# The gated stage's a and b products by one level of Strassen's algorithm on quarter blocks, with partial sums read from one pair of PSUM banks

## The chip, the cores and the metric

The kernel runs on one core of one Trainium2 chip. The metric is the device time of one execution in microseconds (us); three runs were timed and the median is taken. The engines are PE (TensorE, matmuls), ACT (ScalarE), DVE (VectorE), POOL (GpSimd) and SP, which here only issues transfers. Each engine has one queue and works through it in the order written down by the program.

## What is computed

The reference is attention with a bias, then a mixture of four experts, then a gated stage. The change touches the gated stage alone:

```python
# x: 1152 tokens x 512, the experts' output; w_a, w_b: 512 x 1536; w_out: 1536 x 512
a = x @ w_a
b = x @ w_b
return a * b @ w_out
```

## The kernel before

A matrix product keeps a high and a low part of each operand (hi, lo) and adds three PE products, hi*hi + hi*lo + lo*hi; every count of matmuls below has this factor three in it. A matmul holds 128x128 weights (stationary) and streams up to 512 columns (moving).

**Gated stage.** The 1152 tokens are cut into three chunks of 384 and the 1536 inner features into six groups of 256, taken as 2 x 3 (g, q). `ab_item` (line 745) makes one item: for each of two feature halves of 128 it computes a and b, each by `up` (line 677) as 12 matmuls of 384 columns (four blocks of the 512 inputs, times three) into one PSUM bank. ACT copies a out of its bank (line 754), DVE multiplies b with it (756), ACT and DVE split the result into hi and lo (757, 758). `out_item` (line 771) follows one item later: for each of three token tiles `down` (line 689) issues six matmuls of 512 columns; the sum over three groups q stays in the bank `z`, then ACT or DVE moves it to `acc` (782, 784), and the last ones are stored.

**Ahead of it.** `x2_item` (line 732) transposes the experts' output `acc` (36 transposes of 128x128 on PE in all) and ACT and DVE write its hi and lo into `x_hi` and `x_lo`. The weights of the gated stage arrive as 64-bit words; `convert` (line 625) turns them into hi and lo on DVE during the experts' stage and stores them to DRAM (`wz_d`), `unit64` (655) loads them into one of 11 weight buffers `w`.

**What sets the order.** The program lists operations with their dependences; `Plan.run` then makes the queue of every engine from estimated durations and priorities (`RANK`; a lower number goes first), and hands out buffers (`Room`) as earlier users finish. The queues are fixed when the kernel is built; at run time semaphores only hold an instruction back, and all that stands behind it in its queue waits too.

Of the kernel before, what the change touches and what calls it, by code (L numbers as in the profile page):

```python
# [45 lines left out]
SPLIT = True  # L46

# [178 lines left out]
def tile_kernel(ctx, tc, qd, kd, vd, cst, probs, w1r, w2r, war, wbr, wor, out):  # L226
# [43 lines left out]
    solo, attn, hp_stack = ExitStack(), ExitStack(), ExitStack()  # L270
# [3 lines left out]
    R = {z: Room() for z in "w wst h1 h2 u z q2 q k2 k v bt ptb pr rb xf sums rx hh bst asb s64 t64 hl64".split()}  # L274
# [348 lines left out]
    wz_d = dram.tile([2 * NG * NQ + NG * NQ, 2, P, 1024], F32, name="wz_d")  # L623

    def convert(src):
# [3 lines left out]
        for h in range(2):  # L629
# [59 lines left out]
    def down(w, z, h, tt, first, final, prio=RANK["fill"]):  # L689
# [5 lines left out]
        op({"PE": 6 * 226}, mm, r=[w, h], w=[z], prio=prio)  # L695
# [34 lines left out]
    X2 = [Buf(t=x_hi) for _ in range(TOK)]  # L730

    def x2_item(t):
        u = new("u", "px")
        ts = slice(t * P, (t + 1) * P)
        p4 = lambda: u.t.rearrange("p (a b) -> p a b", a=KD)

        def tr(e):
            for d in range(KD):
                nc.tensor.transpose(p4()[:, d, :], acc(t)[:, d * P:(d + 1) * P], ident)  # L739

        op({"PE": 440}, tr, r=[ACC[t]], w=[u], after=ups[t], prio=1)
# [3 lines left out]
    def ab_item(g, c, q):
        h = new("h2", "h")
        if (g, q, "a") not in WU:
            for z in "ab":
                WU[g, q, z] = unit64(UI[g, q, z])
        xs = X2[3 * c:3 * c + 3]  # L750
        for ft in range(2):
            asb = new("asb")
            pa, _ = up(WU[g, q, "a"], ft, c * CH, CH, xs, [h, asb])
            op({"ACT": 490}, lambda e, pa=pa, asb=asb: nc.scalar.copy(asb.t, pa.t[:, :CH]), r=[pa], w=[asb])
            pb, _ = up(WU[g, q, "b"], ft, c * CH, CH, xs, [h, asb])
            op({"DVE": 560}, lambda e, pb=pb, asb=asb: nc.vector.tensor_tensor(out=asb.t, in0=pb.t[:, :CH], in1=asb.t, op=ALU.mult), r=[pb], rw=[asb])  # L756
            hi = op({"ACT": 490}, lambda e, ft=ft, asb=asb: nc.scalar.copy(h.t[0][:, ft, :CH], asb.t), r=[asb], w=[h])  # L757
            op({"DVE": 560}, lambda e, ft=ft, asb=asb: nc.vector.tensor_tensor(out=h.t[1][:, ft, :CH], in0=asb.t, in1=f(h.t[0][:, ft, :CH]), op=ALU.subtract), r=[asb], w=[h], after=[hi], lock=True)  # L758
        return h
# [11 lines left out]
    def out_item(g, c, q, h):  # L771
        if (g, q, "d") not in WU:
            WU[g, q, "d"] = unit64(UI[g, q, "d"])
        for tt in range(3):
            t = 3 * c + tt
            if q == 0:
                ZB[g, c, tt] = new("z", "pz")
            z = ZB[g, c, tt]
            down(WU[g, q, "d"], z, h, tt, q == 0, q == NQ - 1)
            if q == NQ - 1:  # L780
                if g == 0:
                    op({"ACT": 600}, lambda e, z=z, t=t: nc.scalar.copy(acc(t), z.t), r=[z], rw=[ACC[t]])
                else:
                    op({"DVE": 745}, lambda e, z=z, t=t: nc.vector.tensor_tensor(out=acc(t), in0=z.t, in1=acc(t), op=ALU.add), r=[z], rw=[ACC[t]])
                    if g == NG - 1:
                        def put(e, t=t):
                            for r, o, n in rows_of(t):
                                nc.sync.dma_start(out=out[o:o + n, :], in_=acc(t)[r:r + n])
                        op({"SP": 440 * len(rows_of(t))}, put, r=[ACC[t]], size=262144)
# [12 lines left out]
    def chain(items, fu, fd, at=()):  # L802
        prev = None
        for n, key in enumerate(items):
            for t in dict(at).get(n, ()):
                x2_item(t)
            h = fu(*key)
            if prev is not None:
                fd(*prev)
            prev = (*key, h)  # L810
        fd(*prev)

    for p, its in enumerate(PASSES):
        chain([(p, e, c, q) for e in range(E) for c in its for q in range(4)], w1_item, w2_item)
    UI = {}
    for g in range(NG):
        for q in range(NQ):
            for z, src in ("a", war), ("b", wbr), ("d", wor):
                UI[g, q, z] = convert(src[NQ * g + q])
    for t in range(TOK):  # L820
        x2_item(t)
    chain([(g, c, q) for g in range(NG) for c in range(NCH) for q in range(NQ)], ab_item, out_item)


# [25 lines left out]

    ended = lambda o: o.done
# [3 lines left out]
        (lambda: R["bst"].left == 0 and R["hh"].left == 0, bias_end),  # L855
        (lambda: all(o.done for o in fins) and not R["s"].left and not R["tv"].left, attn_end),
# [7 lines left out]
def _layout(q, k, v, w1, b1, w2, moe_domain_probs, moe_w1, moe_w2, moe2_w_a, moe2_w_b, moe2_w_out):  # L864
# [24 lines left out]

    def down(w, n):  # L890
# [36 lines left out]
```

## Time and profile before

| | |
|---|---|
| median of three runs (lowest, highest) | 845.51 us (843.58, 845.67) |
| the profiled execution: its time, its span | 845.99 us, 844.2 us |
| busy in the span: PE, DVE, ACT, POOL | 818.1, 540.2, 327.2, 46.4 us |
| PE busy, 626.33 to 831.60 us (gated stage) | 205.27 of 205.27 us |
| DVE and ACT busy in that stretch | 39.87 and 36.38 us |

The span runs from the first to the last instruction. Matmuls overlap in PE's pipeline, so PE's busy time says that it was never idle, not how fast it went; how fast is read from the distance between the starts of matmuls.

### The profile page before, as it was taken

What the parts mean: (1) busy time and instruction counts of PE and PEld (TensorE: products, weight loads), DVE (VectorE), ACT (ScalarE), POOL (GpSimd) and SP (SyncE); (2) the same over time, 40 slices, a digit from 0 to 9 for tenths busy, and PEclk for the clock granted to TensorE, in tenths of its full rate; (3) what the DMA queues carried; (4) which work ended last, traced back from release to release, by engine and by line L of the source; (5) the groups of instructions that cost most, each with busy time, mean ns of one, the idle gap of its engine ahead of it and who ended that gap; (6) DMA issues with size and microseconds to landing.
All of it is one profiled execution on the core that took longest, in us unless ns stands there. A gap on an engine that the chain in (4) does not pass through costs nothing.

```text
span 844.2 us, 12285 instructions
## 1 busy us (share of the span) xinstructions
PE 818.1 (97%) x4712; PEld 686.2 (81%) x4712; DVE 540.2 (64%) x1052; ACT 327.2 (39%) x640; POOL 46.4 (5%) x53
## 2 busy tenths in 40 slices
PE   6788999999999999999999999999999999999997
PEld 2446776898898788889888888888899999999996
DVE  7998999788888777787978787782421211212222
ACT  6676877577676622332232222121211221211111
POOL 1001100000110000001001000110000000000000
PEclk9999999999999999999999999999999999999999
DMA  6889877576656364566466656746510006201001
GB/s 222 308 272 335 279 253 242 196 237 189 222 174 211 119 228 167 175 207 203 139 228 195 185 160 198 265 140 209 189 51 0 1 1 249 100 1 38 1 38 38
DMA packets 53243, 140.69 MB, mean 167 GB/s; under 512 B 5312, under 2 KB 9408, under 8 KB 53184
## 3 DMA queue, kind: packets, MB, share of 16 engines
q1 hardware_dynamic: 53184, 139.90, 50.7%
q8 instruction: 37, 0.61, 0.3%
q14 instruction: 22, 0.18, 0.1%
HBM read 107.75 MB, written 32.13 MB: 166 GB/s over the span
## 4 chain that ended last, share of the span: by engine, by line
PE 91%; DVE 5%; DMA 3%; issue 1%; ACT 1%; POOL 0%; SPq 0%; DVEq 0%; POOLq 0%
PE up L685 42%; PE pz L694 33%; PE ps L489 5%; PE pv L580 4%; PE pt L515 4%; PE pb L369 2%; DVE hh L355 1%; DMA k<-in_kd 1%; DMA bt<-bias_d 1%; DVE pr L492 1%; DVE ptb L233 1%; PE rp L560 0%; PE px L739 0%; PE pt L532 0%; DMA cs<-in_cst 0%
## 5 line engine op out<-in xcount | busy, mean ns | idle before, releaser
L685 PE MATMUL up<-x_hi,wh 128*128 128x384 f32 (+2 forms) x672 | 230.0, 342 | 0.4 <-DVE hl L711 0.4
L685 PE MATMUL up<-x_hi,wl 128*128 128x384 f32 (+2 forms) x672 | 226.6, 337 | 0.0
L685 PE MATMUL up<-x_lo,wh 128*128 128x384 f32 (+2 forms) x672 | 226.4, 337 | 0.0
L694 PE MATMUL pz<-wh,hh 128*128 128x512 f32 x396 | 157.6, 398 | 0.6 <-ACT hh L757 0.6
L694 PE MATMUL pz<-wl,hh 128*128 128x512 f32 x396 | 156.1, 394 | 0.0
L694 PE MATMUL pz<-wh,hl 128*128 128x512 f32 x396 | 155.8, 393 | 0.1
L685 PEld LDWEIGHTS up<-x_hi,wh 128*128 128x128 f32 x672 | 126.4, 188 | 10.1 <-issue 1.6
L685 PEld LDWEIGHTS up<-x_lo,wh 128*128 128x128 f32 x672 | 126.5, 188 | 6.9
L685 PEld LDWEIGHTS up<-x_hi,wl 128*128 128x128 f32 x672 | 126.4, 188 | 5.7
L756 DVE TENSOR_TENSOR asb<-up,asb 128x384 f32<-128x384 f32 x36 | 20.1, 558 | 144.7 <-PE up L685 144.7
L710 ACT ACTIVATE hh<-up 128x256 fp32r<-128x256 f32 (+2 forms) x96 | 47.1, 491 | 139.5 <-PE up L685 132.2
L694 PEld LDWEIGHTS pz<-wl,hh 128*128 128x128 f32 x396 | 74.3, 188 | 17.2
L694 PEld LDWEIGHTS pz<-wh,hh 128*128 128x128 f32 x396 | 74.5, 188 | 16.2 <-ACT hh L757 1.0
L618 DVE TENSOR_TENSOR wl<-wst,wh 128x1024 fp32r<-128x1024 f32 x64 | 77.8, 1220 | 15.2 <-ACT wh L233 14.9
L694 PEld LDWEIGHTS pz<-wh,hl 128*128 128x128 f32 x396 | 74.4, 188 | 15.1 <-DVE hl L758 0.4
L711 DVE SCALAR_TENSOR_TENSOR hl<-up,hh 128x256 fp32r<-128x256 f32 (+2 forms) x96 | 52.9, 553 | 41.5 <-ACT hh L710 41.0
L233 ACT CAST wh<-wst 128x1024 fp32r<-128x1024 f32 x55 | 57.3, 1045 | 45.8 <-PE pz L694 38.0
L492 DVE CUSTOM_DVE_ANT_0 pr<-ps,bt 128x576 f32<-128x576 f32 (+1 forms) x80 | 59.7, 753 | 12.1 <-PE ps L489 8.5
L502 ACT ACTIVATE pr<-pr,sums 128x576 f32<-128x576 f32 x72 | 55.9, 776 | 12.2 <-DVE sums L492 11.5
L757 ACT CAST hh<-asb 128x384 fp32r<-128x384 f32 x36 | 18.5, 513 | 100.8 <-DVE asb L756 100.8
L369 PE MATMUL pb<-hh,cs 128*32 128x288 f32 (+17 forms) x352 | 47.0, 499 | 6.8 <-DVE hh L355 4.5
L355 DVE TENSOR_SCALAR hh<-cs,negb 128x576 f32<-128x576 f32 (+17 forms) x108 | 49.0, 503 | 0.2
(89 smaller groups left out, 873.3 us busy)
## 6 DMA issues: line engine op xcount, KB each, us to landing
wz_d<-hl SPq DMA_DIRECT2D x36, 512.0 KB, 3.2
wst<-in_w1r SPq DMA_DIRECT2D x32, 512.0 KB, 4.0
wst<-in_w2r SPq DMA_DIRECT2D x32, 512.0 KB, 4.4
bt<-bias_d SPq DMA_DIRECT2D x24, 576.0 KB, 5.5
bias_d<-bst SPq DMA_DIRECT2D x36, 295.5 KB, 4.9
k<-in_kd SPq DMA_DIRECT2D x16, 576.0 KB, 5.1
wh<-wz_d SPq DMA_DIRECT2D x18, 512.0 KB, 3.9
wl<-wz_d SPq DMA_DIRECT2D x18, 512.0 KB, 5.1
```

The costliest lines, as they stand in the source:

```text
L233: (nc.scalar.copy if e == "ACT" else engine[e].tensor_copy)(out, in_)
L355: op({"DVE": n / 1.92 + 240}, lambda e, hh=hh, G=G: nc.vector.tensor_scalar(out=hh.t[:, :n], in0=tab[:, :n], scalar1=sc[:, G:G + 1], scala ...
L369: nc.tensor.matmul(t[32 * g:32 * g + 32, o + lo:o + hi], w2s, hs[g].t[:, lo:hi], start=True, stop=True)
L489: nc.tensor.matmul(ps.t[:, half, o:o + w], lhs, K.t[:, s, k0:k0 + w], start=(kk == 0 and n < 2), stop=(kk == 1 and n in (0, len(runs) - 1)))
L492: nc.vector.tensor_tensor_reduce(out=pr.t[r0:r1, c].rearrange("p (a b) -> p a b", a=2), in0=ps.t[r0:r1, :, :HS], in1=bt.t[r0:r1, c].rearra ...
L502: nc.scalar.activation(out=pr.t[:, c], in_=pr.t[:, c], func=AF.Exp, scale=-1.0, bias=sums.t[:, neg:neg + 1], accum_out=sums.t[:, col:col + 1])
L515: nc.tensor.transpose(pt.t[:, kt * P:kt * P + P], pr.t[:, s, k0:k0 + P], ident)
L618: op(t_two(1024, ENGINES["wlo"]), lambda e: engine[e].tensor_tensor(out=w.t[1], in0=wst.t, in1=f(w.t[0]), op=ALU.subtract), r=[wst], rw=[w ...
L685: nc.tensor.matmul(u.t[:, :n], a[:, d, ft * P:(ft + 1) * P], x[:, d, lo:lo + n], start=(d == 0 and j == 0), stop=(d == 3 and j == 2))
L694: nc.tensor.matmul(z.t, a[:, ft, tt * P:(tt + 1) * P], bb[:, ft, :], start=(first and ft == 0 and j == 0), stop=(final and ft == 1 and j = ...
L710: relu = op({"ACT": n / 1.2 + 170}, lambda en, ft=ft, u=u: nc.scalar.activation(out=h.t[0][:, ft, :n], in_=u.t[:, :n], func=AF.Relu), r=[u ...
L711: op({"DVE": n / 0.96 + 160}, lambda en, ft=ft, u=u: nc.vector.scalar_tensor_tensor(out=h.t[1][:, ft, :n], in0=u.t[:, :n], scalar=0.0, in1 ...
```

## The change

Tokens are now cut in two chunks c of 512 and 640, feature groups are six (q), so there are 12 items (q, c). In an item each of a and b is a product of 2x2 blocks: the weights are cut in two halves of the 512 inputs and two halves of 128 features, the tokens in two halves of n = 256 (c = 0) or 320 (c = 1). Strassen's algorithm (in Winograd's form) needs seven block products for this in place of eight, on sums of blocks. `prod` makes one of them for a and for b: 2 x 6 matmuls of n columns. The pair of banks W collects products 1, 6, 7 and 4 one upon the other and is read in between by ACT (`lift`, l1 to l3); the pair Z collects 5 and 3, V takes product 2. DVE adds these up into `ct` (c11, c22, c12) or multiplies at once (c21), ACT and DVE split the products a*b into hi and lo.

`blocks64` loads a whole (unsplit) weight unit into `wst`, makes four sums of 256 columns on POOL or DVE and splits blocks and sums on ACT and DVE. `x2_pair` makes four differences of token blocks on DVE, and 70 transposes stand for the 36 (14 of them with 64 tokens). `out_item` adds every item's tiles to `acc` by DVE (ACT copies at q = 0), where the sum over three q stayed in the bank before; it comes after product 7 of the next item. Weight buffers `w` are 8 in place of 11.

```diff
             op(t_two(512, ENGINES["s64"]), lambda e, w1=w1, hl=hl: engine[e].tensor_tensor(out=f(w1()), in0=f(w1()), in1=f(hl.t[:, 0]), op=ALU.subtract), r=[hl], rw=[st], prio=RANK["x64"], lock=True)
             op({"DVE": 690}, lambda e, w0=w0, w1=w1, hl=hl: nc.vector.tensor_tensor(out=hl.t[:, 1], in0=f(w1()), in1=f(w0()), op=ALU.add), r=[st], rw=[hl], prio=RANK["x64"], lock=True)
             op({"SP": 440}, lambda e, h=h, hl=hl: nc.sync.dma_start(out=wz_d[k, :, :, 512 * h:512 * h + 512].rearrange("a p n -> p a n"), in_=f(hl.t)), r=[hl], w=[done], prio=2, size=524288)
@@ -661,6 +667,23 @@
 
...
+    def blocks64(k):
+        wst, wa, ws, sm = new("wst"), new("w"), new("w"), new("sum")
+        op({"SP": 440}, lambda e: nc.sync.dma_start(out=wst.t, in_=wz_d[k, 0]), r=[raw64[k]], w=[wst], prio=1, size=524288)
+        a21, a11, a12, a22 = (lambda n=n: wst.t[:, 256 * n:256 * n + 256] for n in range(4))
+        s1, s2, s3, s4 = (lambda n=n: sm.t[n // 2][:, n % 2] for n in range(4))
+        got = []
+        for out, x, y, o in (s1, a21, a22, ALU.add), (s2, s1, a11, ALU.subtract), (s3, a11, a21, ALU.subtract), (s4, a12, s2, ALU.subtract):
+            got.append(op(t_two(256, ENGINES["wsum"]), lambda e, out=out, x=x, y=y, o=o: engine[e].tensor_tensor(out=out(), in0=x(), in1=y(), op=o), r=[wst], w=[sm], after=got, prio=RANK["split2"], lock=True))
+        parts = [(wa, 0, 768, lambda: wst.t[:, 256:], wst, [])]
+        parts += [(ws, 512 * i, 512, lambda i=i: sm.t[i].rearrange("p a b -> p (a b)"), sm, got[:2 * i + 2]) for i in range(2)]
...
+    B11, B21, B22, T1, T2, T3, T4 = range(7)
...
+        for j, x, y in (T1, lambda: a1(0), lambda: a0(0)), (T2, lambda: a1(1), d[T1]), (T3, lambda: a1(1), lambda: a1(0)), (T4, lambda: a0(1), d[T2]):
+            got[j] = op(t_two(W, ENGINES["xsum"]), lambda e, j=j, x=x, y=y: engine[e].tensor_tensor(out=d[j](), in0=x(), in1=y(), op=ALU.subtract), r=src, w=[sm], after={T2: [got.get(T1)], T4: [got.get(T2)]}.get(j, []), prio=RANK["px"], lock=True)
...
+        for j, xs, after in (B11, (lambda: a0(0), lambda: a0(1)), []), (B22, (lambda: a1(1), d[T1]), [got[T1]]), (T2, (d[T2], d[T3]), [got[T2], got[T3]]), (T4, (d[T4],), [got[T4]]):
...
+            def tr(e, u=u, xs=xs):
+                for m, x in enumerate(xs):
+                    for h in range(2):
+                        nc.tensor.transpose(u.t[:, (2 * m + h) * P:(2 * m + h) * P + n], x()[:, h * P:(h + 1) * P], ident[:n, :n])
...
+            to = lambda z, j=j, k=k: xb(c, z)[:, j:j + k, :, cols].rearrange("p j k n -> p (j k) n")
+            px = lambda u=u, k=k: u.t.rearrange("p (a b) -> p a b", b=P)[:, :2 * k, :n]
+            hi = op(t_psum(2 * k * n, "ACT"), lambda e, to=to, px=px: copy(e, to(0), px()), r=[u], w=XB[c][j:j + k], after=every, prio=RANK["px"])
+            op(t_psum(2 * k * n, "DVE"), lambda e, to=to, px=px: nc.vector.tensor_tensor(out=to(1), in0=px(), in1=f(to(0)), op=ALU.subtract), r=[u], w=XB[c][j:j + k], after=[hi], prio=RANK["px"])
...
+    def ab_item(q, c):
+        n = CW[c]
+        for z in "ab":
+            if (q, z) not in WU:
+                WU[q, z] = blocks64(UI[q, z])
+        h, ct = new("h2", "h"), new("ct")
+        W, Z = new("p", "pw"), new("p", "pr")
+        V = new("z", "pq"), new("z", "pq")
+
+        TERMS = {1: (0, B11), 2: (1, B21), 4: (2, T4), 5: (3, T1), 6: (4, T2), 7: (5, T3), 3: (6, B22)}
+
+        def prod(j, bank, first, stop, last=(), hold=()):
+            a, x = TERMS[j]
+            got = []
+            for m, z in enumerate("ab"):
+                w = WU[q, z][a >= 3]
...
+                def mm(e, m=m, w=w):
+                    o_ = bank[m].t[:, :n] if type(bank) is tuple else bank.t[:, m, :n]
+                    wh, wl = (y[:, o:o + 256].rearrange("p (k f) -> p k f", k=2) for y in w.t)
+                    xh, xl = (xb(c, i)[:, x] for i in range(2))
+                    for k in range(2):
+                        for i, (s, d) in enumerate(((wh, xh), (wh, xl), (wl, xh))):
+                            nc.tensor.matmul(o_, s[:, k], d[:, k], start=(first and k == 0 and i == 0), stop=(k == 1 and i == 2), skip_group_check=True)
+
+                got.append(op({"PE": 6 * (n / 2.4 + 11)}, mm, r=[w, XB[c][x]], w=[bank[m] if type(bank) is tuple else bank], hold=hold, after=last, prio=RANK["fill"]))
+            return got
...
+        def lift(i, after):
+            return op(t_psum(2 * n, "ACT"), lambda e: copy(e, slot(i), W.t[:, :, :n]), after=after, hold=[W, ct], prio=RANK["evac2"])
+
+        def plus(i, bank, after):
+            return op(t_psum(2 * n, "DVE"), lambda e: nc.vector.tensor_tensor(out=slot(i), in0=bank.t[:, :, :n], in1=slot(i), op=ALU.add), after=after, hold=[bank, ct], prio=RANK["evac2"])
...
+        m1 = prod(1, W, True, False, hold=[ct, h])
+        l1 = lift(0, m1)
+        m2 = prod(2, V, True, True, m1)
+        c11 = [op(t_psum(n, "DVE"), lambda e, m=m: nc.vector.tensor_tensor(out=ct.t[:, 0, m, :n], in0=V[m].t[:, :n], in1=ct.t[:, 0, m, :n], op=ALU.add), after=[m2[m], l1], hold=[V[m], ct], prio=RANK["evac2"]) for m in range(2)]
+        m6 = prod(6, W, False, False, [l1])
+        l2 = lift(1, m6)
+        m5 = prod(5, Z, True, False, m6)
+        m7 = prod(7, W, False, False, [l2, *m5])
+        l3 = lift(3, m7)
+        c22 = plus(3, Z, [*m5, l3])
+        m4 = prod(4, W, False, True, [l3])
+        l4 = op(t_psum(n, "ACT"), lambda e: copy(e, ct.t[:, 2, 0, :n], W.t[:, 0, :n]), after=m4[:1], hold=[W, ct], prio=RANK["evac2"])
+        c21 = op(t_psum(n, "DVE"), lambda e: nc.vector.tensor_tensor(out=ct.t[:, 2, 0, :n], in0=W.t[:, 1, :n], in1=ct.t[:, 2, 0, :n], op=ALU.mult), after=[l4, *m4], hold=[W, ct], prio=RANK["evac2"])
+        m3 = prod(3, Z, False, True, [c22, *m4])
+        gap[:] = m7
+        c12 = plus(1, Z, [l2, *m3])
+
...
+        split(1, [c21, times(3, 1, [c22])])
+        split(0, [times(0, 2, [*c11, c12])])
...
+    AB = [(q, c) for q in range(NQ) for c in ((0, 1) if q < NQ - 1 else LASTC)]
...
+            if (q, c) != AB[-1]:
+                down(WU[q, "d"], z, h, tt, True, True, after=gap)
...
+                for ft in (1, 0):
...
+                    halves.append(op({"PE": 3 * 226}, mm, r=[WU[q, "d"]], w=[z], hold=[h], prio=RANK["fill"], after=[*parts[q, c, ft], *halves]))
...
+                op({"ACT": 600}, lambda e, z=z, t=t: nc.scalar.copy(acc(t), z.t), r=[z], rw=[ACC[t]], prio=RANK["evac2"])
+            else:
+                op({"DVE": 745}, lambda e, z=z, t=t: nc.vector.tensor_tensor(out=acc(t), in0=z.t, in1=acc(t), op=ALU.add), r=[z], rw=[ACC[t]], prio=RANK["evac2"])
...
     for p, its in enumerate(PASSES):
...
+    def banks(n, side):
+        place(R["z"], tp(ctx, f"ps_z{n}", space=PSUM, side=side), f"z{n}", 2, [P, 512])
+        place(R["u"], tp(stacks[n], f"ps_u{n}", space=PSUM, side=side), f"u{n}", 2, [P, 512], mark="u")
...
+        for n, side in enumerate(("right", "left")):
+            stacks[n].close()
+            place(R["p"], tp(ctx, f"ps_p{n}", space=PSUM, side=side), f"p{n}", 1, [P, 2, 512])
...
+    def converted_end():
+        cv_stack.close()
+        place(R["ct"], tp(ctx, "ct"), "ct", 2, [P, 4, 2, W2])
```

**Order on ACT, at the end of a long item (c = 1) and the start of the next short one (c = 0).** Before, in a stretch of the gated stage (`asb` is the copied a, `up` a bank, `hh` the hi part, `acc` the result; brackets name the semaphores waited for):

```order
L754 COPY asb_6740<-up_6743 128x384 [waits PE_49,Activation_49]
L782 COPY acc3_4049<-pz_6614 128x512 [waits PE_49]
L782 COPY acc4_4063<-pz_6622 128x512 [waits PE_49]
L782 COPY acc5_4357<-pz_6629 128x512 [waits PE_49]
L757 CAST hh_6741<-asb_6740 128x384 [waits DVE_49]
L754 COPY asb_6760<-up_6761 128x384 [waits PE_49,Activation_49]
```

Now, from items (1,1) to (2,0) (`pw` is the pair W, `wh` and `wst` hi part and raw weights of a later unit, `sumh` and `suml` weight sums):

```order
L234 COPY ct_6798<-pw_6799 128x320 [waits PE_49]
L234 CAST wh_6922<-sumh_6639 128x512 [waits Pool_49]
L234 CAST wh_6922<-suml_6640 128x512 [waits Pool_49]
L234 CAST hh_6800<-ct_6798 128x320 [waits DVE_49]
L234 CAST hh_6800<-ct_6798 128x256
L234 CAST hh_6800<-ct_6798 128x64
L234 CAST wh_6958<-wst_6695 128x768 [waits DMAHW0_49,PE_49]
L234 COPY ct_6939<-pw_6940 128x2x256 [waits PE_49,Activation_49]
L234 CAST wh_6981<-sumh_6734 128x512 [waits PE_49]
L234 CAST wh_6981<-suml_6735 128x512
L234 COPY ct_6939<-pw_6940 128x2x256 [waits PE_49]
```

The rows `ct_6939<-pw_6940` are l1 and l2 of item (2,0): casts of weights, one of which waits for a load and one for POOL, now stand in the queue ahead of them.

**Order on DVE at the same place.** Before, around a multiplication:

```order
L758 TENSOR_TENSOR hl_7617<-asb_7635,hh_7616 128x384 [waits Activation_49]
L756 TENSOR_TENSOR asb_7700<-up_7712,asb_7700 128x384 [waits PE_49,Activation_49]
L758 TENSOR_TENSOR hl_7702<-asb_7700,hh_7701 128x384 [waits Activation_49]
L756 TENSOR_TENSOR asb_7720<-up_7728,asb_7720 128x384 [waits PE_49,Activation_49]
L758 TENSOR_TENSOR hl_7702<-asb_7720,hh_7701 128x384 [waits Activation_49]
L784 TENSOR_TENSOR acc6_4386<-pz_7656,acc6_4386 128x512 [waits PE_49]
```

Now (line 859 is c21, which frees W; 845 is c12; 850 the two c11; `wl` and `hl` are lo parts, `pr` is Z, `pq` is V):

```order
L859 TENSOR_TENSOR ct_6798<-pw_6799,ct_6798 128x320 [waits Activation_49]
L685 TENSOR_TENSOR wl_6923<-sumh_6639,wh_6922 128x512 [waits Activation_49]
L685 TENSOR_TENSOR wl_6923<-suml_6640,wh_6922 128x512 [waits Activation_49]
L878 TENSOR_TENSOR hl_6801<-ct_6798,hh_6800 128x320 [waits Activation_49]
L878 TENSOR_TENSOR hl_6801<-ct_6798,hh_6800 128x256 [waits Activation_49]
L878 TENSOR_TENSOR hl_6801<-ct_6798,hh_6800 128x64 [waits Activation_49]
L680 TENSOR_TENSOR sumh_6971<-wst_6795 128x256 [waits DMAHW1_49,DVE_49]
L845 TENSOR_TENSOR ct_6798<-pr_6848,ct_6798 128x640 [waits PE_49]
L850 TENSOR_TENSOR ct_6939<-pq_6974,ct_6939 128x256 [waits PE_49,Activation_49]
L850 TENSOR_TENSOR ct_6939<-pq_6986,ct_6939 128x256 [waits PE_49]
L865 TENSOR_TENSOR ct_6798<-ct_6798 128x2x320 [waits DVE_49]
```

Work on weights and the additions of the Strassen products now share DVE's queue with the splits that the next `down` needs. On PE, six of the 14 groups of six product matmuls of an item begin with a wait on ACT or DVE.

## Rows read from the trace of the kernel before

**Rows 1.** The page's part 1: busy us (share of the span) xinstructions.

```profile
PE 818.1 (97%) x4712; PEld 686.2 (81%) x4712; DVE 540.2 (64%) x1052; ACT 327.2 (39%) x640; POOL 46.4 (5%) x53
```

**Rows 2.** Windows: stretch, length, busy us of PE, PEld, DVE, ACT, POOL, clock, DMA share.

```profile
626.33:831.60 205.27, 205.27 (x1075) 191.57 (x1075) 39.87 (x70) 36.38 (x74) 0.00 (x0) 1.00 0.12 44
592.80:626.33 33.53, 33.12 (x182) 29.79 (x181) 13.16 (x20) 8.55 (x16) 0.00 (x0) 1.00 0.39 130
```

**Rows 3.** All waits of PE from 296 to 845 us: total, times, longest.

```profile
PE pz L694 <- ACT hh L757: 0.6, 1, 0.6
PE px L739 <- DVE acc L728: 0.4, 1, 0.4
```

**Rows 4.** The chain that ended last, gated stage: start us, us, what.

```profile
630.69 8.48 PE up L685 x48
...
681.08 8.38 PE up L685 x48
689.46 4.12 PE pz L694 x18
...
819.22 8.35 PE up L685 x48
```

**Rows 5.** Timeline, PE, first chunk of the experts: start us, us (256 columns).

```profile
148.55 0.28 PE L685 MATMUL up<-x_hi,wl 128*128 128x256 f32 x1
...
150.33 0.28 PE L685 MATMUL up<-x_hi,wl 128*128 128x256 f32 x1
```

**Rows 6.** Weight loads by shape, whole span: busy us, mean ns.

```profile
L685 PEld LDWEIGHTS up<-x_lo,wh 128*128 128x128 f32 x672 | 126.5, 188 | 6.9
```

**Rows 7.** Timeline, PE, around transposes ahead of the gated stage.

```profile
596.01 0.39 PE L685 MATMUL up<-x_hi,wl 128*128 128x512 f32 x1
596.24 1.03 PE L739 MATMUL px<-ident,acc 128*128 128x128 f32 x8
...
597.34 0.39 PE L685 MATMUL up<-x_lo,wh 128*128 128x512 f32 x1
```

**Rows 8.** Timeline, PE, a group of six that opens late.

```profile
140.28 0.36 PE L685 MATMUL up<-x_hi,wh 128*128 128x256 f32 x1
140.48 0.28 PE L685 MATMUL up<-x_lo,wh 128*128 128x256 f32 x1
```

**Rows 9.** Groups by shape on ACT and DVE: busy us, mean ns | idle before.

```profile
L754 ACT COPY asb<-up 128x384 f32<-128x384 f32 x36 | 17.3, 479 | 74.8 <-PE up L685 74.8
L233 ACT COPY ptb<-pt 128x512 f32<-128x512 f32 x44 | 25.3, 584 | 15.1 <-PE pt L515 14.9
L233 ACT CAST wh<-wst 128x1024 fp32r<-128x1024 f32 x55 | 57.3, 1045 | 45.8 <-PE pz L694 38.0 <-DMA wst<-in_w1r 6.8 <-DMA wst<-in_w2r 0.9
L756 DVE TENSOR_TENSOR asb<-up,asb 128x384 f32<-128x384 f32 x36 | 20.1, 558 | 144.7 <-PE up L685 144.7
L784 DVE TENSOR_TENSOR acc<-pz,acc 128x512 f32<-128x512 f32 x9 | 6.2, 692 | 14.8 <-PE pz L694 14.8
L618 DVE TENSOR_TENSOR wl<-wst,wh 128x1024 fp32r<-128x1024 f32 x64 | 77.8, 1220 | 15.2 <-ACT wh L233 14.9
```

**Rows 10.** Timeline, all engines, the last item.

```profile
834.61 0.34 PE L685 MATMUL up<-x_hi,wl 128*128 128x384 f32 x1
...
835.25 0.40 PE L694 MATMUL pz<-wl,hh 128*128 128x512 f32 x1
...
836.18 0.56 DVE L758 TENSOR_TENSOR hl<-asb,hh 128x384 fp32r<-128x384 f32 x1 [0.58 <-ACT hh L757]
...
837.14 0.39 PE L694 MATMUL pz<-wl,hh 128*128 128x512 f32 x1
```

**Rows 11.** Transfers by line: count, KB each, median us to landing.

```profile
wst<-in_w1r SPq DMA_DIRECT2D x32, 512.0 KB, 4.0
wl<-wz_d SPq DMA_DIRECT2D x18, 512.0 KB, 5.1
```

More of the change, by code (lines that the diff above doesn't have):

```diff
@@ L26 @@
 F2 = 1536
-NG, NQ = 2, 3
-CH = 384
-NCH = NT // CH
+NQ = 6
 TOK = NT // P
@@ L46 @@
 SPLIT = True
+X2AT = 2
+LASTC = (0, 1)
 def f(ap):
@@ L687, in up, with down @@
         return u, got[-1]
-    def down(w, z, h, tt, first, final, prio=RANK["fill"]):
+    gap = []
+    def down(w, z, h, tt, first, final, prio=RANK["fill"], after=()):
         def mm(e):
@@ L745, in ab_item @@
[L745 to L758, printed above, removed]
+    B11, B21, B22, T1, T2, T3, T4 = range(7)
@@ L776, in out_item, with put @@
             if q == 0:
-                ZB[g, c, tt] = new("z", "pz")
-            z = ZB[g, c, tt]
-            down(WU[g, q, "d"], z, h, tt, q == 0, q == NQ - 1)
+                op({"ACT": 600}, lambda e, z=z, t=t: nc.scalar.copy(acc(t), z.t), r=[z], rw=[ACC[t]], prio=RANK["evac2"])
+            else:
+                op({"DVE": 745}, lambda e, z=z, t=t: nc.vector.tensor_tensor(out=acc(t), in0=z.t, in1=acc(t), op=ALU.add), r=[z], rw=[ACC[t]], prio=RANK["evac2"])
             if q == NQ - 1:
[L781 to L789, printed above, removed]
+                def put(e, t=t):
+                    for r, o, n in rows_of(t):
+                        nc.sync.dma_start(out=out[o:o + n, :], in_=acc(t)[r:r + n])
+                op({"SP": 440 * len(rows_of(t))}, put, r=[ACC[t]], size=262144)
@@ L804, in chain @@
         for n, key in enumerate(items):
-            for t in dict(at).get(n, ()):
-                x2_item(t)
+            if n in dict(at):
+                dict(at)[n]()
             h = fu(*key)
@@ L830, in experts_room @@
         solo.close()
-        for z in "uz":
-            place(R[z], tp(ctx, f"ps_{z}", space=PSUM, side="right"), z, 2, [P, 512])
+        banks(0, "right")
     def bias_end():
@@ L855, in tile_kernel @@
         (lambda: R["bst"].left == 0 and R["hh"].left == 0, bias_end),
+        (lambda: R["h1"].left == 0, first_end),
+        (lambda: all(o.done for o in every_up), gated_begin),
+        (lambda: R["u"].gone == 4, gated_room),
+        (lambda: all(o.done for o in converted), converted_end),
         (lambda: all(o.done for o in fins) and not R["s"].left and not R["tv"].left, attn_end),
@@ L904, in _layout @@
         "w1r": up(moe_w1, 4), "w2r": down(moe_w2, 4),
-        "war": words(up(moe2_w_a, 6)), "wbr": words(up(moe2_w_b, 6)), "wor": words(down(moe2_w_out, 6)),
+        "war": words(blocks(moe2_w_a)), "wbr": words(blocks(moe2_w_b)), "wor": words(down(moe2_w_out, 6)),
     }
```

147 lines of the change are left out of this document (107 added, 40 removed).

## The prediction

> **What bounds the kernel now.** I read the shares of busy time first: PE is busy for 97% of the span, DVE for 64%, ACT for 39% [rows 1]. That is an average over stages, so the windows come next. In the gated stage, from 626.33 to 831.60 us, PE is never idle, while DVE works 40 and ACT 36 of 205 us, and the clock is at 1.00, the higher of its two levels (2.4 GHz) [rows 2]. Then the waits of PE: from 296 us to the end there are two, 1.0 us in all [rows 3]. So the time of this stage is PE's own pace, and a change counts by the matmuls that it saves and by the waits that it brings. The pace is read in the chain of waits: 48 matmuls of 384 columns take 8.38 us (the middle of three rows, 8.35 to 8.48), or 0.1746 us each, and the pieces repeat with little spread. From 630.69 to 819.22 us lie 15 items, 12.57 us each; less 8.38 us this leaves 4.19 us for 18 matmuls of 512 columns, 0.2328 us each [rows 4].
>
> **What is removed and added on PE.** Before: 18 items x 48 = 864 product matmuls, 864 x 0.1746 = 150.9 us. After: six short items (n = 256) and six long ones (n = 320), each with 7 products x 12 = 84 matmuls, so 504 of each length. The 256-column pace stands in the experts' first chunk: 15 starts from 148.55 to 150.33 us, 0.1187 us each [rows 5]. For 320 columns there is no row. Five sixths of the 384-column pace is 0.1455 us, midway between 256 and 384 is 0.1467 us; I take 0.146. Then 504 x 0.1187 + 504 x 0.146 = 59.8 + 73.6 = 133.4 us, a saving of 17.5 us. If both lengths cost strictly by column, 0.1164 and 0.1455 us, the saving is 18.9 us; it is 17.1 us at 0.1467. The `down` matmuls stay 324 of 512 columns.
>
> A shorter matmul would lose its gain if a weight load could not hide behind it. A load takes 188 ns [rows 6], longer than the 118.7 ns between two 256-column starts [rows 5], and each of these has its own load: the loads overlap the stream, and PE keeps nearly the pace of its columns. From 256 to 512 columns the start distance grows by 114.1 ns, 0.446 ns a column, which leaves a fixed part of 4.6 ns per matmul [rows 4, 5]. A rule speaks against this. The Trainium skill, TensorE: Matmul & The Clock Gate, section Back-to-back issue gap, gives sustained spacings of about 81 ns at 128 columns and 131 ns at 512, a fixed part of some 64 ns by my estimate. By those figures 864 matmuls of 384 columns would cost 99 us and the 1008 shorter ones 103 us, so the change would lose 4 us. The trace disagrees: 232.8 ns at 512 columns, not 131.
>
> **Transposes.** Eight of them stretch the distance from the last product's start at 596.01 to the second one behind them at 597.34 us to 1.33 us; two 512-column paces are 0.466, so eight cost 0.87 us, 0.109 each [rows 7]. There are 34 more, 3.7 us; 14 of the 70 have 64 tokens, and if these cost half it is 2.9 us. I take 3.4.
>
> **What ACT and DVE get, and what hides it.** W is read three times while later products wait to be added to it. A lift is a copy of 512 (short item) or 640 columns (long): 0.584 us, and by the slope from 384 columns (0.479) some 0.69 us [rows 9]. Behind l1 PE has product 2, behind l2 product 5, 12 matmuls each: 1.42 or 1.75 us. Behind l3 it has four or five tiles of `down`, at least 5.6 us. With 0.1 us of handoff at either end the lifts fit, unless ACT is held by something else. I walked the tightest place, from a long item to a short one, with the start of product 4 as 0. Product 4 ends at 1.75. The multiplication c21 must free W: 0.49 us on DVE, done by 2.4. Product 3's first half covers until 2.63, so the margin is 0.2 us. ACT meanwhile casts two weight sums, three parts of `hh` and 768 weight columns (0.8 us by the 1024-column row) and reaches l1 at about 4.5, done at 5.1; product 6 begins at 6.33. DVE does c12, both c11, the long multiplication and two weight splits, and writes the first part of `hl` at 10.0; the first `down` begins at 10.6. So nothing waits in this walk, with margins of 0.2, 1.2 and 0.6 us.
>
> Summed per q, DVE has 24.5 us: 5.2 for the short item, 6.7 for the long one, 9 x 0.69 for `acc`, 6.4 for two weight units (columns at 1.04 ns, by the 384, 512 and 1024 rows) [rows 9]. PE needs 42 x (0.1187 + 0.146) x 2 + 54 x 0.2328 = 34.8 us. DVE is 70% full where it was 19%, ACT about 35%. I allow 0.1 us per item for margins missed, 1.2 us, and 0.5 us in the first item, where DVE has about 15.5 us (12 differences x 0.43, twelve writes of transposed blocks of 128 to 512 columns with 6.6 together, 3.7 for the item itself) beside about 16 us on PE (42 transposes, 4.6; the item's products, 10.0; the next one's first, 1.75). Together 1.7 us; bounds are 0 and, since a group that opens late pays 0.08 us (0.20 against 0.12 between its first two starts [rows 8]) and six groups per item begin with a wait, 12 x 6 x 0.08 = 5.8 us. Weight units now load into two buffers shortly ahead of use; such loads land in 4 to 5 us [rows 11], against 17 us of PE work in each item, and the stage moved little data [rows 2]. I cost them at nothing; if that cover fails, the cast that waits for them stands ahead of l1.
>
> **The end.** Before, the last `hl` came late: 1.89 us lie between the starts at 835.25 and 837.14, three paces are 0.70, so 1.19 us are lost [rows 10]. Now the halves of the last tiles whose factors are ready come first, 4 x 0.70 us of cover for c12, a multiplication, a cast and a split (0.83 + 0.83 + 0.46 + 0.49, with handoffs about 3.0, behind some 0.5 us of older splits); I expect a loss of 0.4, so 0.8 us gained, between -0.4 and 1.2.
>
> **Sum.** -17.5 + 3.4 + 1.7 - 0.8 = -13.2 us. Against the profiled execution (845.99 us) this gives 832.8; the median of the runs shown is 0.5 us lower, so I forecast 832.3 us. About 0.3% (2.5 us) is what a measurement can tell from no change.
>
> **Rivals.**
> - DVE sets the pace in places: its queue is 70% full and in order, so a c22, c12 or `hl` behind a weight split arrives late and `down` or product 3 waits. If each item loses 0.6 us, 7 us are gone: about 839. For it: the first item's tight balance; against it: 0.6 us of margin in the walk, and ACT, whose copies feed these steps, is only 35% full. Chance 0.12.
> - Slower than before: the lifts lie bare. Their place is ACT's queue, where casts that wait for a weight load, for POOL's sums or for a freed buffer stand ahead of l1 and l2, as the order on ACT shows. A bare lift costs its copy and two handoffs, 0.78 or 0.89 us; 18 of each are 30 us, so 862 at worst. It decides from 0.37 us per lift on (13.2 / 36). At two thirds it is 852. Before, such casts did wait for loads, 7.7 us over 55 of them [rows 9]; against it stand 1.2 us of margin and the quiet DMA [rows 2]. Chance 0.10.
> - A fixed cost per matmul: with 64 ns of the 384-column pace fixed, 256 columns would cost 138 ns and 320 ones 156 ns, the saving would be 2.8 us and the time 847. The Trainium skill's spacings (the section named above) are the rule behind it. The 256-column row, 118.7 ns, excludes it unless short matmuls run slower beside full PSUM traffic. Chance 0.02.
> - The change fails to leave work out: excluded by PE's order, which holds 84 matmuls per item. Other losses that land within 0.3%: 0.04.
>
> **How the numbers follow.** The forecast has 0.72; with its own bounds (saving 18.9 to 17.1, transposes 2.9 to 3.7, waits 0 to 5.8, end 1.2 to -0.4) it runs from 828 to 838. The range reaches on to 841 for the DVE rival and leaves out the other 0.16 and the forecast's edges. Faster: 0.72 + 0.12 = 0.84. Same: 0.04 + 0.02 = 0.06. Slower: 0.10.
>
> **What would show it.** Right: products of 256 columns about 0.119 and of 320 about 0.146 us apart; an item pair of 34.8 us with no wait of PE above 0.2 us; lifts that end while product 2, product 5 or `down` still runs; DVE near 70% in the stage. Wrong: waits of PE on a `ct` written by ACT (lifts), on `hl` or `ct` by DVE (the DVE rival), on weights by DMA, or short matmuls well above 0.12 us apart.

## The result, and the profile after

The changed kernel takes 834.15 us (median of four runs, 833.18 to 834.46); the kernel before, on the same chip, 844.68 us. The ratio is 0.9874, 95% interval [0.9856, 0.9891]: faster by 1.26%, 1.8 us above the forecast of 832.3 and inside the range. The profiled executions took 834.46 us after and 845.99 us before, their spans 832.7 and 844.2 us: 11.5 us between the spans, where the sum said 13.2. Of these, 1.4 us lie ahead of the experts' stage: the first matmul of the experts starts at 93.91 us before and at 92.47 after, and at 91.69 to 93.33 us in the seven other versions below, although ACT, DVE and POOL do the same work in the same order up to 88 us in all nine traces.

```profile
93.91 0.28 PE L685 MATMUL up<-x_hi,wh 128*128 128x256 f32 x1
...
92.47 0.28 PE L708 MATMUL up<-x_hi,wh 128*128 128x256 f32 x1
```

From the experts on, the changed kernel is 10.1 us shorter.

The page's part 1, busy time by engine, against [rows 1]:

```profile
PE 806.7 (97%) x4890; PEld 672.2 (81%) x4890; DVE 626.3 (75%) x1221; ACT 349.8 (42%) x687; POOL 52.1 (6%) x72
```

PE has 178 matmuls more and 11.4 us less to do; DVE works 86 us longer. Windows against [rows 2], with the same columns (stretch, length, busy us of PE, PEld, DVE, ACT, POOL, clock, DMA share, GB/s): the transposes with the first products, the next items, then the steady part.

```profile
607.02:635.37 28.35, 28.21 (x205) 26.40 (x205) 21.89 (x43) 12.32 (x24) 6.36 (x8) 1.00 0.09 25
635.37:687.47 52.10, 51.77 (x332) 47.59 (x331) 30.53 (x61) 22.91 (x46) 3.54 (x5) 1.00 0.24 74
687.47:817.63 130.16, 129.45 (x806) 119.00 (x806) 75.05 (x134) 35.74 (x70) 7.63 (x10) 1.00 0.13 43
```

PE is busy for over 99% of each, at clock 1.00. In the last row DVE works 58% and ACT 27% of the time. All waits of PE from 296 us to the end, against [rows 3], are now in one row:

```profile
PE pw L834 <- DVE ct L859: 1.0, 6, 0.2
```

Line 859 is c21, the multiplication that frees the pair W: product 1 of the next item waits for it, five times after a long item and once after a short one. The chain of waits around the first of them (start us, us, what; a piece is counted from the end of the one before it, and a matmul still runs when the next has started, so first starts lie some 0.16 us earlier):

```profile
640.97 1.78 PE pw L834 x12
642.75 0.02 issue
642.77 0.43 ACT ct L234
643.20 0.02 issue
643.23 0.50 DVE ct L859
643.73 0.04 issue
643.77 1.70 PE pw L834 x12
645.47 0.89 PE pr L834 x6
646.36 1.43 PE pq L834 x12
647.79 1.41 PE pw L834 x12
```

The first row is product 4 of the first long item, 640.97 to 642.75. Behind it ACT copies half of W (l4), DVE multiplies (c21), and only then product 1 of the next short item starts, at 643.77. The rest is PE alone; 12 matmuls of 256 columns take 1.41 to 1.43 us, 0.118 each. The timeline shows what PE had as cover, and what ACT was doing:

```profile
641.55 0.31 PE L834 MATMUL pw<-x_hi,wl 128*128 128x320 f32 x1
...
642.43 0.31 PE L834 MATMUL pw<-x_hi,wl 128*128 128x320 f32 x1
642.57 0.31 PE L834 MATMUL pr<-x_hi,wh 128*128 128x320 f32 x1
...
642.77 0.42 ACT L234 COPY ct<-pw 128x320 f32<-128x320 f32 x1 [1.18 <-PE pw L834]
```

The cover, six matmuls of product 3, begins at 642.57 and is worth 0.88 us, so product 1 is due at 643.45: 0.32 us are lost, and another 0.10 at its slow start (its first two matmuls lie 0.22 us apart in place of 0.118). ACT had been idle for 1.18 us when it began l4, though the half of W that l4 reads was complete after six of product 4's twelve matmuls (the first two rows are the sixth and the twelfth), about 0.9 us before the second half. l4 began 0.04 us behind the end of the second, and so it does in all twelve items.

### The profile page after: what moved, and what is told of

Same layout as the page of the kernel before. It is cut to its first block, busy times and chain, and to the rows that moved or that the text cites. A ratio compares the mean times of both kernels' runs of the same rounds, so it can differ in the third digit from the quotient of the medians.

```text
span 832.7 us, 12785 instructions
## 1 busy us (share of the span) xinstructions
PE 806.7 (97%) x4890; PEld 672.2 (81%) x4890; DVE 626.3 (75%) x1221; ACT 349.8 (42%) x687; POOL 52.1 (6%) x72
## 4 chain that ended last, share of the span: by engine, by line
PE 90%; DVE 5%; DMA 3%; ACT 1%; issue 1%; DVEq 0%
PE pz L719 32%; PE up L708 24%; PE pw L834 9%; PE ps L490 5%; PE pv L581 4%; PE pr L834 4%; PE pt L516 4%; PE pq L834 2%; PE pb L370 2%; DMA k<-in_kd 1%; DVE hh L356 1%; DMA bt<-bias_d 1%; PE pz L911 1%; PE px L798 1%; DVE ptb L234 1%
## 5 line engine op out<-in xcount | busy, mean ns | idle before, releaser
L719 PE MATMUL pz<-wh,hl 128*128 128x512 f32 x386 | 151.6, 393 | 0.0
L708 PE MATMUL up<-x_hi,wh 128*128 128x256 f32 (+2 forms) x384 | 133.2, 347 | 0.4 <-DVE hl L736 0.4
L708 PE MATMUL up<-x_hi,wl 128*128 128x256 f32 (+2 forms) x384 | 129.8, 338 | 0.0
L708 PE MATMUL up<-x_lo,wh 128*128 128x256 f32 (+2 forms) x384 | 129.7, 338 | 0.0
L234 ACT CAST wh<-wst 128x1024 fp32r<-128x1024 f32 (+1 forms) x66 | 66.3, 1007 | 93.0 <-PE pz L719 73.7
L708 PEld LDWEIGHTS up<-x_hi,wh 128*128 128x128 f32 x384 | 72.4, 188 | 9.5 <-issue 1.6
L708 PEld LDWEIGHTS up<-x_lo,wh 128*128 128x128 f32 x384 | 72.4, 189 | 6.4
L708 PEld LDWEIGHTS up<-x_hi,wl 128*128 128x128 f32 x384 | 72.3, 188 | 5.9
L234 ACT COPY ct<-pw 128x512 f32<-128x512 f32 (+3 forms) x48 | 27.8, 579 | 105.5 <-PE pw L834 105.1
L493 DVE CUSTOM_DVE_ANT_0 pr<-ps,bt 128x576 f32<-128x576 f32 (+1 forms) x80 | 59.7, 754 | 11.4 <-PE ps L490 8.4
L516 PE MATMUL pt<-ident,pr 128*128 128x128 f32 x288 | 43.6, 280 | 2.6 <-ACT pr L503 2.4
```

What stands on the lines that cost most here:

```text
L234: (nc.scalar.copy if e == "ACT" else engine[e].tensor_copy)(out, in_)
L493: nc.vector.tensor_tensor_reduce(out=pr.t[r0:r1, c].rearrange("p (a b) -> p a b", a=2), in0=ps.t[r0:r1, :, :HS], in1=bt.t[r0:r1, c].rearra ...
L516: nc.tensor.transpose(pt.t[:, kt * P:kt * P + P], pr.t[:, s, k0:k0 + P], ident)
L708: nc.tensor.matmul(u.t[:, :n], a[:, d, ft * P:(ft + 1) * P], x[:, d, lo:lo + n], start=(d == 0 and j == 0), stop=(d == 3 and j == 2))
L719: nc.tensor.matmul(z.t, a[:, ft, tt * P:(tt + 1) * P], bb[:, ft, :], start=(first and ft == 0 and j == 0), stop=(final and ft == 1 and j = ...
```

## Experiments

Two theories stood after this. **A**: PE's own pace sets the time, and c21's wait comes from l4 starting behind all of product 4. **B**: the lifts or DVE's queue hold PE. Losses of PE below are start distances less the pace of the matmul, summed from 590 us to the end (4.7 us in the changed kernel, 0.6 of them in the last item). A span is that of one execution; a difference "from the experts on" leaves out what lies ahead of their first matmul.

**Product 1 later.** Product 1 of the next item waits for both halves of product 3, so that the whole of product 3 covers l4 and c21.

```diff
-        m1 = prod(1, W, True, False, hold=[ct, h])
+        m1 = prod(1, W, True, False, last=tuple(prev3), hold=[ct, h])
...
+        prev3[:] = m3
```

> Only the order of PE's queue changes: the next item's product 1 waits for both halves of product 3, where at six item boundaries it stood between them. Theory A (the changed kernel is bound by PE's pace, and its one real loss in the stage is product 1 waiting for c21 to free W, 0.32 us of idle and 0.10 us of restart at six places): these six waits go, no new one comes, 2.5 us less than the changed kernel, about 831.6 us median. Theory B (DVE's queue is what is late; the wait only shows where PE first meets it): the wait moves to product 6 or to the down tiles, and the time stays within 1 us of 834.2.

Measured: 832.55 us, ratio 0.9859 [0.9839, 0.9878], span 830.3; from the experts on 1.6 us less than the changed kernel. The times themselves overlap (831.64 to 834.36 here, 833.18 to 834.46 there), so the trace has to tell. No wait of PE is listed any more, and its losses fall to 3.1 us: the six are gone, but, against what theory A expected, four of about 0.18 us appear before product 6. Only product 2 is then left between product 1 and it, and l1 stands behind three casts of weights on ACT: in the first such place it ends at 646.54, and product 6 starts at 646.59. The order alone gives back some of the loss, and costs part of it elsewhere.

**Two tiles.** W and Z become two tiles of one bank each, in place of one tile of two banks; the lifts and additions over both become two instructions each. Dependences and order of the products stay; on PE the trace has the same products and transposes in the same order, matmul by matmul.

```diff
...
-            return op(t_psum(2 * n, "ACT"), lambda e: copy(e, slot(i), W.t[:, :, :n]), after=after, hold=[W, ct], prio=RANK["evac2"])
+            return op(t_psum(2 * n, "ACT"), lambda e: [copy(e, slot(i)[:, m], W.t[m][:, :n]) for m in range(2)], after=after, hold=[W, ct], prio=RANK["evac2"])
...
-        l4 = op(t_psum(n, "ACT"), lambda e: copy(e, ct.t[:, 2, 0, :n], W.t[:, 0, :n]), after=m4[:1], hold=[W, ct], prio=RANK["evac2"])
+        l4 = op(t_psum(n, "ACT"), lambda e: copy(e, ct.t[:, 2, 0, :n], W.t[0][:, :n]), after=m4[:1], hold=[W, ct], prio=RANK["evac2"])
...
```

> W and Z are each two one-bank tiles in place of one two-bank tile; every lift and every addition of a pair becomes two instructions of n columns. The order of the queues stays. Theory A1 (the copy l4 of the first half of product 4 is late by one half, 0.7 to 0.9 us, because its wait is kept per tile and both halves lie in one): l4 starts right behind the first half, c21 ends about 0.65 us after product 4, the six waits of product 1 go, and the time falls by about 2.5 us, less what the longer lifts cost (each 0.15 to 0.2 us longer, hidden): 831.5 to 832.5 us. Theory A2 (l4 is late for another reason, such as ACT being busy): l4 still starts after the second half, the waits stay at about 0.42 us each, 834 us or a little more.

Measured: **830.76 us** (830.47 to 831.36, five runs), ratio 0.9837 [0.982, 0.9854], span 828.7; from the experts on 3.5 us less than the changed kernel. The timeline at the same place (`pwa` and `pwb` are the halves of W, `pra` the first of Z):

```profile
640.10 0.31 PE L834 MATMUL pwa<-x_hi,wh 128*128 128x320 f32 x1
...
640.99 0.31 PE L834 MATMUL pwb<-x_hi,wh 128*128 128x320 f32 x1
...
641.18 0.42 ACT L234 COPY ct<-pwa 128x320 f32<-128x320 f32 x1 [0.29 <-PE pwa L834]
...
642.13 0.49 DVE L859 TENSOR_TENSOR ct<-pwb,ct 128x320 f32<-128x320 f32 x1 [4.95 <-ACT wh L234]
...
642.75 0.40 PE L834 MATMUL pwa<-xb,wh 128*128 128x256 f32 x2
```

l4 now starts 1.08 us after product 4's first matmul and ends before product 4's second half does. c21 is done at 642.62, and product 1 follows product 3's last start at its pace. No wait of PE is listed; losses are 1.3 us. So in the changed kernel l4 waited for the whole tile, whose second bank it does not read; A holds. This version beats both kernels.

**Eight products.** Product 2 is made twice, the second time over the first, so that an item has as many products as the ordinary method.

```diff
-        m2 = prod(2, V, True, True, m1)
+        m2 = prod(2, V, True, False, m1)
+        m2 = prod(2, V, True, True, m2)
```

> Product 2 is made twice (the first result is overwritten by the second), so an item has eight products, as a plain product of 2x2 blocks has; all else of the change stays. Theory A (PE's pace bounds): 72 more matmuls of 256 and 72 of 320 columns at 0.118 and 0.1467 us, 12 x 6 x 2 in all, are 72 x 0.118 + 72 x 0.1467 = 19.1 us more than the changed kernel, 853 us, so 8 to 9 us slower than the kernel before; the longer cover may give back a few tenths. Theory B (DVE bounds in places): the added work falls partly into idle time, and the time grows by 14 us or less, to 848 or below.

Measured: 853.46 us, ratio 1.0104 [1.0078, 1.0129], span 851.4; from the experts on 19.1 us more than the changed kernel. Twelve items times 12 matmuls at 0.118 or 0.1467 us are 19.1. Nothing hid the extra product: PE's pace bounds the stage. Without the saved product the change would make the kernel slower by 9 us.

**Bare lift.** Product 5 goes ahead of product 6, so nothing lies between the lift l2 and product 7, which adds onto W.

```diff
-        m6 = prod(6, W, False, False, [l1])
+        m5 = prod(5, Z, True, False, m2)
+        m6 = prod(6, W, False, False, [l1, *m5])
         l2 = lift(1, m6)
-        m5 = prod(5, Z, True, False, m6)
-        m7 = prod(7, W, False, False, [l2, *m5])
+        m7 = prod(7, W, False, False, [l2])
```

> Product 5 is made ahead of product 6, so that nothing lies between product 6 and product 7, which waits for the lift l2. Theory A: l2 is hidden by product 5 alone, so it now lies bare, 0.59 or 0.69 us of copy, 0.1 us of handoffs and 0.1 us of restart in each of 12 items: 6 x 0.79 + 6 x 0.89 = 10 us more, about 844 us; PE waits for ACT's copy out of W 12 times with 0.6 to 0.8 us each. Rival: the waits show but the time is given back at c21 or at the end because another queue sets the pace: less than 5 us more.

Measured: 854.42 us, ratio 1.0115 [1.009, 1.014], span 852.8; from the experts on 20.4 us more than the changed kernel, twice what was expected. The waits of PE:

```profile
PE pw L834 <- ACT ct L234: 9.4, 13, 0.8
PE px L798 <- DVE suml L788: 1.5, 2, 0.9
PE px L798 <- DVE x_lo L804: 1.3, 3, 0.9
PE pw L834 <- DVE ct L859: 1.2, 7, 0.2
PE px L798 <- DVE sumh L788: 1.2, 2, 0.8
```

The lift costs 0.93 us per short and 1.04 per long item with the slow start behind it, 11.8 us in twelve items; the thirteenth wait of the first row is l1 of the first item, bare there as well. The rest lies in the first item: with the new order the planner packed the transposes (px) together, and they waited for DVE's differences. Windows there, as above:

```profile
611.00:621.50 10.50, 6.58 (x46) 4.76 (x44) 10.44 (x25) 5.59 (x12) 0.00 (x0) 0.99 0.00 1
621.50:624.90 3.40, 3.29 (x15) 3.20 (x16) 1.83 (x4) 1.57 (x3) 2.79 (x4) 0.50 0.00 0
624.90:628.00 3.10, 3.10 (x17) 3.10 (x16) 2.65 (x3) 0.05 (x1) 3.10 (x4) 0.50 0.23 20
```

PE idles for 3.9 of 10.5 us while DVE is hardly ever free, and then the granted clock is 0.50, the lower level (1.2 GHz), until 628.0. The chain shows its price (start us, us, what):

```profile
622.06 2.86 PE pq L834 x12
624.91 2.56 PE pr L834 x12
627.47 1.72 PE pw L834 x12
```

Two products that take 1.42 us each elsewhere take 2.86 and 2.56 us, 2.6 us more.

**Bare lift, from the third item on.** As before, but the first two of twelve items keep the order of the changed kernel; this parts the lift from the first item.

```diff
-        m6 = prod(6, W, False, False, [l1])
-        l2 = lift(1, m6)
-        m5 = prod(5, Z, True, False, m6)
-        m7 = prod(7, W, False, False, [l2, *m5])
+        if (q, c) in AB[:2]:
+            m6 = prod(6, W, False, False, [l1])
+            l2 = lift(1, m6)
+            m5 = prod(5, Z, True, False, m6)
+            m7 = prod(7, W, False, False, [l2, *m5])
+        else:
+            m5 = prod(5, Z, True, False, m2)
+            m6 = prod(6, W, False, False, [l1, *m5])
+            l2 = lift(1, m6)
+            m7 = prod(7, W, False, False, [l2])
```

> As e4_bare_lift (product 5 ahead of product 6, so that nothing lies between l2 and product 7), but the first two items keep the changed kernel's order; 16 of 18 items have the bare lift. Theory: e4 lost 0.93 us per short and 1.04 us per long item by the lift, and the rest of its 20 us, some 8 us, in the first item, where the planner bunched the transposes and the granted clock then fell to 0.50. Then this kernel loses 8 x 0.93 + 8 x 1.04, at most 16 us, and as e4 listed 13 such waits of 18, more likely 10 to 12 us: 844 to 846 us, with the granted clock at 1.00 all through the stage and no stretch of PE below 90 per cent from 612 to 622 us. Rival: the loss at the first item belongs to the bare lift itself and moves to another item, with a stretch at 0.50: 850 us or above.

Measured: 844.66 us (ten runs), ratio 1.0 [0.9986, 1.0013], span 843.4; from the experts on 10.1 us more than the changed kernel. The text on record counts 18 items, so its range was met by luck; there are 12, ten of them with the bare lift, so 5 x 0.93 + 5 x 1.04 = 9.9 us were due. That is what PE's losses grew by, 4.7 to 14.6 us. The row of waits has ten:

```profile
PE pw L834 <- ACT ct L234: 7.3, 10, 0.8
```

The chain shows the first of them: product 6 ends, ACT copies, product 7 follows:

```profile
650.00 1.42 PE pw L834 x12
...
651.43 0.59 ACT ct L234
...
652.07 1.69 PE pw L834 x12
```

The window of the first item has PE busy again and the clock at 1.00:

```profile
607.02:621.50 14.48, 14.41 (x105) 13.20 (x104) 9.92 (x20) 6.52 (x13) 0.00 (x0) 1.00 0.01 2
```

The two versions lie 10.3 us apart; two bare lifts less are 2.0 of it, so 8.3 of the 20.4 us before, some two fifths, came from the first item and not from l2. Each bare lift eats what the change gains per item (10.5 us over twelve items, 0.9 each): ten bare lifts make it a draw.

**Lifts twice.** Each lift is made twice on ACT.

```diff
-            return op(t_psum(2 * n, "ACT"), lambda e: copy(e, slot(i), W.t[:, :, :n]), after=after, hold=[W, ct], prio=RANK["evac2"])
+            o = op(t_psum(2 * n, "ACT"), lambda e: copy(e, slot(i), W.t[:, :, :n]), after=after, hold=[W, ct], prio=RANK["evac2"])
+            return op(t_psum(2 * n, "ACT"), lambda e: copy(e, slot(i), W.t[:, :, :n]), after=[o], hold=[W, ct], prio=RANK["evac2"])
```

> The copies l1 to l3 that lift W into ct are each made twice on ACT, 36 + 18 copies of 512 or 640 columns more (0.584 us and some 0.69 us, 34 us of ACT work in all); nothing else is changed. Cover theory: l1 ended 1.37 us and l2 0.6 us ahead of the products that wait for them in the changed kernel, l3 several us ahead; a second copy of 0.6 to 0.7 us in front then leaves l1 hidden and l2 on its edge. So at most 18 x 0.1 = 2 us more than the changed kernel, 834 to 836 us, and any new wait of PE stands before product 7. Rival, ACT's queue is on its edge: every l1 and l2 comes 0.6 us late, 36 x 0.6 = 22 us more, 856 us.

Measured: 838.79 us, ratio 0.9926 [0.9903, 0.9948], span 837.1; from the experts on 3.6 us more than the changed kernel, for 21.0 us of ACT work (370.8 against 349.8 busy; 36 copies, not the 54 of the text). Neither number expected was met, though it is near the lower. The chain shows why:

```profile
663.54 1.94 PE pw L834 x12
...
665.50 0.70 ACT ct L234
666.20 0.51 ACT hh L234
666.71 0.60 ACT ct L234
...
667.36 2.04 PE pw L834 x12
```

Product 1 ends at 665.48, and product 6 may start at 667.36, 1.88 us later. The planner had put a cast of `hh` between the two copies. By the starts, product 6 comes 0.30 us later than product 2's pace would have it, and loses 0.11 more at its slow start. There are nine such places of 0.26 to 0.30 us: five before product 7, as expected, and four before product 6 in long items. A tenth, of 0.74 us, lies in the first item, where the planner also moved products. So even three ACT instructions in a row outlast their cover by 0.3 us only. The single lift has room.

**Splits twice.** The low part of each split of the products' weights is made twice on DVE.

```diff
-            op(t_two(n, ENGINES["wlo2"]), lambda e, w=w, o=o, n=n, x=x: engine[e].tensor_tensor(out=w.t[1][:, o:o + n], in0=x(), in1=f(w.t[0][:, o:o + n]), op=ALU.subtract), after=[hi], hold=[b], w=[w], prio=RANK["split2"], lock=True)
+            lo_ = op(t_two(n, ENGINES["wlo2"]), lambda e, w=w, o=o, n=n, x=x: engine[e].tensor_tensor(out=w.t[1][:, o:o + n], in0=x(), in1=f(w.t[0][:, o:o + n]), op=ALU.subtract), after=[hi], hold=[b], w=[w], prio=RANK["split2"], lock=True)
+            op(t_two(n, ENGINES["wlo2"]), lambda e, w=w, o=o, n=n, x=x: engine[e].tensor_tensor(out=w.t[1][:, o:o + n], in0=x(), in1=f(w.t[0][:, o:o + n]), op=ALU.subtract), after=[lo_], hold=[b], w=[w], prio=RANK["split2"], lock=True)
```

> The low part of each split of the weight units of products (a subtraction on DVE) is made twice, about 28 us of DVE work more in the gated stage, where DVE is 58 per cent busy; nothing else is changed. Cover theory: DVE's queue has room, so at most 2 us more than the changed kernel, 834 to 836 us. DVE rival: its queue is in order and sets the pace in places, a c22, c12 or low part of hl behind a doubled split comes late: 5 us more or above, 839 us up.

Measured: 835.13 us, ratio 0.9889 [0.987, 0.9908], span 832.5; from the experts on 0.5 us more than the changed kernel, and within the cover theory's 834 to 836 us. Its steady window and its only waits:

```profile
687.47:817.63 130.16, 129.46 (x805) 118.97 (x804) 87.07 (x153) 35.27 (x70) 14.71 (x13) 1.00 0.14 45
```

```profile
PE pw L835 <- DVE ct L860: 1.0, 6, 0.2
```

DVE does 24.4 us more in all and is 67% busy here, and PE waits as before. DVE's queue does not set the time; B falls for it as for the lifts.

## Why the prediction was right, and where its sum was off

**The bound.** Right: PE alone carries the stage, and an eighth product costs its full 19.1 us.

**The saving, 17.5 us.** Right. 256 columns cost 0.118 us (predicted 0.1187) and 320 columns, 12 in 1.76 us in the chain, 0.1467 (predicted 0.146): 504 x (0.118 + 0.1467) = 133.4 us, the forecast's own figure.

```profile
663.78 1.76 PE pq L834 x12
```

The step from 256 to 320 columns is 28.7 ns, 0.448 a column, much as the 0.446 from 256 to 512 before. This leaves about 3 ns fixed per matmul and ends the rival of a large fixed cost. By the Trainium skill's spacings (TensorE: Matmul & The Clock Gate, Back-to-back issue gap) the fixed part would be some 64 ns by my estimate, and the products no cheaper than before; no row here shows it.

**The lifts.** Right. The trace at the walk's place, with the start of product 4 at 640.81:

```profile
640.81 0.31 PE L834 MATMUL pw<-x_hi,wh 128*128 128x320 f32 x1
...
645.68 0.58 ACT L234 COPY ct<-pw 128x512 f32<-128x512 f32 x1
647.63 0.40 PE L834 MATMUL pw<-xb,wh 128*128 128x256 f32 x2
649.24 0.59 ACT L234 COPY ct<-pw 128x512 f32<-128x512 f32 x1 [1.79 <-PE pw L834]
650.37 0.96 DVE L878 TENSOR_TENSOR hl<-ct,hh 128x320 fp32r<-128x320 f32 x3
650.44 0.40 PE L834 MATMUL pw<-xb,wh 128*128 128x256 f32 x2
651.85 0.40 PE L719 MATMUL pz<-wh,hh 128*128 128x512 f32 x1
```

The walk had l1 done at 5.1 and product 6 at 6.33; the trace has 5.45 and 6.82, a margin of 1.4 (walk: 1.2). l2 of that item ended at 649.83, product 7 began at 650.44: 0.6. All three parts of `hl` were done at 651.33, `down` began at 651.85: 0.5 (walk: 0.6, for the first part). The slower rival priced a bare lift at 0.78 or 0.89 us; measured with the slow start it is 0.93 or 1.04, so that all 36 bare would have cost 35 us, not 30. Its two handoffs of 0.1 us, for which it names no row, were near: by the starts, product 7 comes 0.83 us late behind a bare copy of 0.59, and the slow start of 0.10, which the price left out, comes on top.

**The step that failed.** "The multiplication c21 must free W: 0.49 us on DVE, done by 2.4. Product 3's first half covers until 2.63, so the margin is 0.2 us." In the trace, from the same zero, c21 is done at 2.92 and product 1 starts at 2.96, where product 3's first half covers until 2.64. DVE took its 0.50 us; what was wrong is the copy ahead of it. The walk has no term for l4, and its 2.4 leaves room for it only beside product 4's second half; l4 ran behind both halves, 0.43 us on the path with a handoff at either end. The version with two tiles shows the cause: with the same products in the same order, l4 runs beside the second half, and the six waits are gone. Its median is 3.4 us lower, of which the six places make 2.6; the rest are single places around the transposes of the first item and in the last item, whose cause was not followed up.

**Waits, 1.7 us allowed.** Too low. PE lost about 4.1 us ahead of the last item: 2.6 at c21 in six places (0.32 or 0.38 and a slow start of 0.10 each), and some 1.5 in single slow starts of 0.08 to 0.11, many around the transposes of the first item. The bounds, 0 to 5.8, hold it, and the upper bound's 0.08 us for a late group [rows 8] is near the 0.08 to 0.11 of each.

**The end.** 0.6 us were lost against 1.19 before; 0.4 was forecast.

**The sum.** From the experts on the change is worth 10.1 us, 3.1 less than the sum said. Added up from the distances between the starts of matmuls in that stretch, the gated products save 13.8 us: 17.5 by their pace, less 3.7 of waits and slow starts among them, for which 1.7 was allowed. The transposes cost 3.1 (forecast 3.4). The experts' `up` matmuls of 512 columns, among which the early transposes now stand, take 0.7 more, for which the sum had no term. `down` with the end gains 0.3 (forecast 0.8). Another 0.2 us lie elsewhere. That the forecast time is off by 1.8 us only is in part luck: the execution before from which it was counted reached the experts 1.4 us later than the one after.

**DVE.** Forecast 70% full and harmless, it was 58% in the steady part, and at 67% still harmless. The DVE rival (839 us) named the right engine in the row of waits for the wrong reason: c21 was late because its input was. The weight loads, put at nothing, cost nothing: no wait of PE on one is listed.

## What to carry to other kernels

Where PE's pace sets the time, a saved product is worth its full matmul time, but only while each read of a running sum has a product of its own as cover: here one bare read per item gave the gain back. Give banks that are filled and read at different times tiles of their own, even if this takes more instructions; a wait can be for the tile and not for the part that is read. When an order is changed for a test, look at what else the planner moved before the loss is put down to the test.

## What was not expected of the hardware

The granted clock fell to 0.50 without any long pause of PE. In the first version with the bare lift PE had been busy for 6.58 of 10.50 us, each listed wait was at most 0.9 us, and it then ran at the lower level until 628.0, which cost some 2.6 us on top of the waits. From 612.17 to 621.9 us PE did nothing but transposes, so this does not tell whether the many short waits or the transposes among them were the reason. With the transposes spread between products, in the changed kernel and in the second such version, the clock stayed at 1.00.
